# Ten-token group moved to the end of the order, with its first matmul in one pass of seven products

## The chip, the cores and the metric

One Trainium2 chip, one core of it. The metric is the device time of one execution in microseconds (us). Of the kernel before, three runs were timed: 951.03, 950.65 and 1230.56, median 951.03.

## The reference

The input x has 8 batches of 4224 tokens of 192 features. A causal convolution of seven taps runs along the tokens; its weights are softmaxed and shared by 24 features (eight heads). Then comes a block that normalizes each token, multiplies by 192x768, takes the relu, multiplies by 768x192 and adds the result to its input:

```python
w = np.exp(weight - max); w = w / (sum(w) + 1e-09)
out[b, s, h, :] = sum_k w[h, k] * x_pad[b, s + k, h, :]      # K = 7, zeros ahead of each batch
xn = (x - mu) / np.sqrt(var + 1e-06) * g_ln                  # x is now out
return x + np.maximum(xn @ w_ch1, 0.0) @ w_ch2
```

All is float32.

## The kernel before

**Groups.** The 33792 tokens lie on 128 partitions in 264 columns, and the work goes in 18 groups of columns. Group 0 has 6 columns of batch 0, group 1 the 8 columns that are left over of all batches, group 2 the next 10 columns of batch 0, and groups 3 to 17 have J = 16 columns each. The list is `groups` (L70).

**One group.** Its x is loaded with six earlier tokens a partition (`load_x`, L133; two buffers). The first tap is a multiplication on ScalarE (ACT, `first_tap`), the second one too, into a tile of its own that DMAs of the POOL queue add to y (`second_tap`, `add_second_tap`, L400 to L407). The other taps are multiply-adds on VectorE (DVE), one for each tap and head (`conv`, L409, 40 in a group). DVE turns y round in 32x32 blocks (`transpose`, yt) and takes its moments. GpSimd (POOL) works out the root of the variance for two groups at a time (`root`, chained by `chain_of`), in a generator whose halves are put between other POOL work. y is stored to the output, and the block's result is later added to it there by accumulating DMAs (`add_to_out`).

**The first matmul ("up").** Groups 0 to 2 go through `up` (L559): for each of six blocks of 128 hidden features, 24 matmuls with 32x128 weights, four side by side, evicted by ACT with the relu. Groups 3 to 17 go through `up_mixed` (L617), which splits both operands in quarters and makes seven products of quarters instead of eight. It does so in two passes, `one` over one block of features a half and `two` over two, with two sets of four PSUM banks, X and Y, by turns. Each pass starts on the set that the other pass did not end with, so pass two starts and ends on Y. The products need sums of quarters: of the weights (`w1sums`, made once by POOL), and of y (`sums_of_y`, L599: two by DVE, two by POOL). Evictions are on ACT, additions into already evicted quarters are DMAs of the POOL queue or DVE additions from PSUM (`close`, L662 to L670; the last of them, of c21, is DVE's L666). The taps of the next group stand on DVE's queue between these (`taps_of_next`, L744 to L777).

**The second matmul ("down").** Groups 0 and 1 go through `down` (L798), with 128x128 weights. From group 2 on, `down_fast` (L842) makes seven products over as many columns as `fast` gives: 10 in group 2, 16 in the full groups, 12 in the last one, whose other four columns are plain (`down_row`, L796). The half sums for it are written over the quarters that they are made of (`half_sum`). ACT work of the next groups is put behind its products (`work`, `behind`).

**The order around the change.** It is written out by hand in the loop at the end (L1016 to L1085). Every engine runs its instructions in the order in which they are issued, and so do the DMA queues of SP and POOL. At L1026 to L1062 the first three groups are woven together: during group 0 the taps of groups 1 and 2 are begun, the load of group 3 goes out on SP (`load_x(3, gate=True)`, L1041), then eight stores of group 1 (`store_y(1)`). During group 1 DVE makes group 2's ten columns (`conv(2, 2)`, L1047), POOL makes `w2sums` (L1051 to L1054), and group 3 is begun. During group 2's first matmul DVE makes most of group 3's taps (L1058, L1060). In the last group the evictions of pass one are shared by ACT and DVE (L648 to L656), and the group before is scaled by DVE (L731 to L736).

Of the kernel before, what the change touches and what calls it, by code (L numbers as in the profile page):

```python
# [16 lines left out]
def kernel(  # L17
# [52 lines left out]
    groups = [(0, 0, 6), (None, 0, LEFT), (0, 6, J - 6), (0, J, J)]  # L70
    groups += [(b, j0, J) for b in range(1, B) for j0 in (0, J)]
    assert PAD <= 6 and max(n for _, _, n in groups) <= J
# [3 lines left out]
    fast = {g: groups[g][2] if g >= 3 else 0 for g in range(NG)}  # L76
    fast[NG - 1] = J - 4
    fast[2] = groups[2][2]
# [3 lines left out]
    MIXED = range(3, NG)  # L82
    PAIR = NF // 2 - 1
    HJ = J // 2
    EARLY = 10
# [47 lines left out]
    def load_x(g, queue=nc.sync, pad=True, gate=False):  # L133
# [21 lines left out]
        if b:  # L155

            queue.dma_start(
                out=flat[:, 0 : (PAD + n) * D],
                in_=bass.AP(
                    tensor=x.tensor, offset=(b * S - PAD) * D, ap=[[R * D, P], [1, (PAD + n) * D]]  # L160
                ),
            )
            if pad:
                nc.gpsimd.memset(t[0:1, 0:PAD, :], 0.0)
            return
# [215 lines left out]

    def second_tap(g, heads=(0, H)):

        n = groups[g][2]
        if heads[0]:
            pass
        elif g == 2:
            part = upool.tile([P, 3 * HJ * CH * C], F32, tag="ys", name="tb2")
            tb[g] = part[:, 0 : n * D].rearrange("p (j d) -> p j d", d=D)
        elif g == 3:  # L390
            tb[g] = room[:, (NF * NQ * C - D) * J :].rearrange("p (j d) -> p j d", d=D)
        else:
            tb[g] = bpool.tile([P, J, D], F32, tag="tb", name=f"tb{g}")
        for h in range(*heads):
            cs = slice(h * GRP, h * GRP + GRP)
            nc.scalar.mul(tb[g][:, 0:n, cs], xg[g][:, 1 : 1 + n, cs], taps[:, h, 1:2])  # L396
        if heads[1] == H:
            add_second_tap(g)

    def add_second_tap(g, upto=H):  # L400
        n = groups[g][2]
        step = 4 if upto == H else 8
        for js in (slice(j, min(j + step, n)) for j in range(0, n, step)):
            ends = [v[:, js, 0 : upto * GRP] for v in (y[g], tb[g])]
            if upto == H:
                ends = [v.rearrange("p j d -> p (j d)") for v in ends]
            nc.gpsimd.dma_start(out=ends[0], in_=ends[1], accum_op=ALU.add)  # L407
# [24 lines left out]
    def chain_of(g):  # L432


        return g - g % 2 if g < 3 else g - 1 + g % 2
# [55 lines left out]
    def hidden_tile(g):  # L491
        n = groups[g][2]

        if fast[g]:
            ht[g] = room.rearrange(
                "p (h e f q j t) -> p h e f q j t", h=2, e=2, f=FC, q=NQ, t=width(g)
# [10 lines left out]
    def evict_up(g, f, src):  # L507

        if not fast[g]:
            dst = ht[g][:, f].rearrange("p j q t -> p q j t")  # L510
            src = src.rearrange("p q (j t) -> p q j t", t=C)
        elif width(g) == C:
            dst = of_products(g)[:, :, f // FC, f % FC].rearrange("p h q j t -> p q h (j t)")
            src = src.rearrange("p q (h w) -> p q h w", h=2)
        else:
            dst = ht[g][:, :, f // FC, f % FC].rearrange("p h q j t -> p q j h t")
            src = src.rearrange("p q (j h t) -> p q j h t", h=2, t=T)
            for q in range(NQ):
                nc.scalar.activation(dst[:, q], src[:, q], AF.Relu)
            return  # L520
        nc.scalar.activation(dst, src, AF.Relu)  # L521
# [23 lines left out]
    def between(g, f):  # L545

        if g == 1 and f > 2:
            second_tap(3, heads=[(0, 2), (2, 5), (5, 6)][f - 3])
        elif g == 2:
            if f == 0:  # L550
                scale(0, 0, groups[0][2])
                add_to_out(0, 0, groups[0][2])
                nc.gpsimd.memset(xg[4][0:1, 0:PAD, :], 0.0)
            elif f == 2:
                add_to_out(1, 0, groups[1][2])
            elif f > 2:
                first_tap(4, heads=[(0, 3), (3, 6), (6, 7)][f - 3])
# [34 lines left out]
    def quarters_of_y(g):  # L592
        if width(g) == C:
            cuts = [(slice(HJ * h, HJ * h + HJ), slice(0, C)) for h in range(2)]
        else:
            cuts = [(slice(0, J), slice(T * h, T * h + T)) for h in range(2)]
        return [yt[g][:, js, CH * k : CH * k + CH, ts] for js, ts in cuts for k in range(2)]

    def sums_of_y(g, engine):  # L599
# [3 lines left out]
        s1, s2, s3 = [room[:, v] for v in range(3)]  # L603
        a11, a12, a21, a22 = quarters_of_y(g)
        ysums[g] = s1, s2, s3, a21
# [6 lines left out]
        engine.tensor_tensor(a21, a12, s2, op=ALU.subtract)  # L612
# [4 lines left out]
    def up_mixed(g, ahead, pending):  # L617
# [3 lines left out]
        last = g + 1 == NG  # L621
# [5 lines left out]
        done = groups[g - 1][2]  # L627

        class Pass:
            def __init__(self, f0, f1, chain, other):  # L630
                self.n, self.chain, self.other = f1 - f0, chain, other
# [14 lines left out]
            def evict(self, banks, dst, relu=False, f=None):  # L646
                src = self.seen(banks, f)
                if last and self.n == 1:  # L648
                    near, far = [[v[:, :, q : q + 2] for v in (dst, src)] for q in (0, 2)]
                    if relu:  # L650
                        nc.scalar.activation(*near, AF.Relu)
                        nc.vector.tensor_scalar_max(*far, 0.0)
                    else:
# [462 lines left out]
```

## Time and profile before

The profile is of one execution on core 0.

| | |
|---|---|
| span of the profiled execution | 948.1 us |
| median of the runs | 951.03 us, 2.9 above that span |
| granted TensorE clock, mean | 1.000 |
| DVE taps, L415, 128x384 | 602, pace 0.53 us |
| group 2: first matmul, second matmul on PE | 19.59, 17.43 us |
| full group: first matmul, second matmul | 27.61, 27.33 us |
| last group: second matmul of 12 columns, four plain columns | 20.73, 8.01 us |
| last DVE instruction starts | 944.03 us |
| accumulating DMA y<-tb, 384 KB, issue to landing | 8.4 us median |
| load of x of a full group, 2112 KB, issue to landing | 16.2 us median |

In the lines of the profile, PE is the matmul engine and PEld its weight loads, DVE is VectorE, ACT is ScalarE, POOL is GpSimd, SP the queue that issues DMAs. L531 is every matmul of `up` and `up_mixed`, L859 every one of `down_fast`, L796 every one of `down_row`. Each matmul stands in the records twice, so 252 matmuls are 504 records. A line of a timeline has start, duration, engine, line, operation, out<-in, shapes and count, and in brackets the idle time before it with what ended it.

### The profile page before, as it was taken

The numbers are of one execution on the slowest core, as the hardware profiler recorded it, in microseconds if no ns is written. First come the engines' busy times: TensorE is split into PE (matmuls) and PEld (weight loads), VectorE is DVE, ScalarE is ACT, GpSimd is POOL, SyncE is SP. The second block draws the span as 40 slices with busy tenths as digits, with TensorE's granted clock in tenths as the row PEclk, the third lists the DMA queues.
The fourth block names the chain that finished last, engine by engine and source line by source line (L and its number), as shares of the span: only waits on it lengthen the run. The fifth ranks groups of instructions, "written<-read, shape, count | busy, mean of one in ns | idle before, by whom it ended". The sixth has DMA issues, their size and how long they took to land.

```text
span 948.1 us, 38092 instructions
## 1 busy us (share of the span) xinstructions
PE 940.8 (99%) x16910; PEld 751.7 (79%) x16910; DVE 893.7 (94%) x1498; ACT 699.8 (74%) x1250; POOL 342.7 (36%) x478
## 2 busy tenths in 40 slices
PE   8999999999999999999999999999999999999998
PEld 7998896877869687786968898696877869696787
DVE  8999999999999999999999999999999999999867
ACT  6764678596877969687896968779696877867362
POOL 2158422723145141533227141452316341261420
PEclk9999999999999999999999999999999999999999
DMA  8359589689797988979698896969889797778261
GB/s 222 97 151 220 102 235 274 121 190 231 135 270 134 252 162 188 220 132 279 126 252 151 199 221 127 282 131 251 162 194 213 131 274 136 174 137 131 54 114 68
DMA packets 39833, 169.35 MB, mean 179 GB/s; under 512 B 4469, under 2 KB 8182, under 8 KB 33655
## 3 DMA queue, kind: packets, MB, share of 16 engines
q0 software_dynamic: 32992, 107.46, 61.1%
q1 hardware_dynamic: 6672, 59.47, 17.0%
q8 instruction: 132, 2.16, 0.9%
q14 instruction: 31, 0.25, 0.1%
q10 hardware_dynamic: 6, 0.00, 0.0%
HBM read 38.93 MB, written 50.33 MB: 94 GB/s over the span
## 4 chain that ended last, share of the span: by engine, by line
PE 96%; DMA 2%; POOL 1%; ACT 1%; issue 0%; SPq 0%; DVE 0%; ACTq 0%; POOLq 0%
PE ps L531 46%; PE ps L859 44%; PE ps L796 4%; DMA xg<-in_x_dram 1%; DMA room<-room 1%; PE ps L326 1%; ACT room L660 0%; POOL room L615 0%; PE ps L352 0%; POOL d L458 0%; ACT w L360 0%; ACT room L521 0%; POOL r L481 0%; POOL d L476 0%; POOL d L477 0%
## 5 line engine op out<-in xcount | busy, mean ns | idle before, releaser
L415 DVE SCALAR_TENSOR_TENSOR y<-xg,taps,y 128x384 f32<-128x384 f32 (+3 forms) x720 | 364.2, 581 | 2.4 <-DMA y<-room 1.9
L859 PE MATMUL ps<-room,w2sums 128*32 128x256 f32 (+2 forms) x4608 | 245.5, 371 | 0.2 <-issue 0.2
L531 PE MATMUL ps<-yt,w 32*128 32x256 f32 (+2 forms) x4160 | 237.6, 373 | 0.1
L531 PEld LDWEIGHTS ps<-yt,w 32*128 32x128 f32 x4160 | 210.3, 185 | 21.9 <-issue 7.0
L859 PEld LDWEIGHTS ps<-room,w2sums 128*32 128x32 f32 x4608 | 154.7, 110 | 84.9 <-issue 0.8
L660 ACT COPY room<-ps 128x512 f32<-128x512 f32 (+1 forms) x213 | 174.2, 859 | 62.9 <-PE ps L531 62.4
L859 PE MATMUL ps<-room,w 128*32 128x256 f32 (+2 forms) x3456 | 189.2, 371 | 0.0
L826 DVE TENSOR_TENSOR room<-room 128x1024 f32<-128x1024 f32 (+2 forms) x147 | 161.2, 1169 | 21.5 <-PE ps L859 11.1
L859 PEld LDWEIGHTS ps<-room,w 128*32 128x32 f32 x3456 | 113.9, 110 | 67.2 <-DVE room L666 5.0
L531 PE MATMUL ps<-ysums,w1sums 32*128 32x256 f32 x2160 | 127.0, 376 | 0.2 <-issue 0.2
L531 PEld LDWEIGHTS ps<-ysums,w1sums 32*128 32x128 f32 x2160 | 116.2, 185 | 5.4 <-issue 0.6
L949 POOL DMA_DIRECT2D out_dram<-ot x69 | 59.0, 940 | 162.8 <-ACT ot L938 159.2
L865 ACT COPY cs<-ps 128x256 f32<-128x256 f32 (+2 forms) x192 | 70.3, 368 | 45.1 <-PE ps L859 45.0
L407 POOL DMA_DIRECT2D y<-tb x59 | 52.2, 1375 | 137.8 <-ACT room L865 104.6
L673 ACT ACTIVATE room<-room 128x1024 f32<-128x1024 f32 (+1 forms) x89 | 94.4, 1073 | 2.9 <-DMA room<-parts_cs 2.8
L938 ACT ACTIVATE ot<-ot,r 128x192 f32<-128x192 f32 x224 | 94.7, 468 | 0.0
L378 ACT ACTIVATE y<-xg,taps 128x384 f32<-128x384 f32 (+3 forms) x141 | 73.0, 607 | 0.5 <-DMA xg<-in_x_dram 0.5
L446 DVE BATCH_NORM_STATS2 st<-y 128x6 f32<-128x192 f32 x264 | 70.1, 343 | 0.0
L531 PE MATMUL ps<-yt,w1sums 32*128 32x256 f32 x1080 | 68.9, 376 | 0.1
L865 ACT COPY room<-ps 128x256 f32<-128x256 f32 (+2 forms) x96 | 35.4, 370 | 45.0 <-PE ps L859 44.1
L531 PE MATMUL ps<-ysums,w 32*128 32x256 f32 x1080 | 68.3, 374 | 0.0
L396 ACT ACTIVATE tb<-xg,taps 128x384 f32<-128x384 f32 (+1 forms) x120 | 66.1, 628 | 0.0
(120 smaller groups left out, 935.7 us busy)
## 6 DMA issues: line engine op xcount, KB each, us to landing
xg<-in_x_dram SPq DMA_DIRECT2D x14, 2112.0 KB, 16.2
room<-room POOLq DMA_DIRECT2D x45, 512.0 KB, 5.2
out_dram<-ot POOLq DMA_DIRECT2D x59, 384.0 KB, 9.3
y<-tb POOLq DMA_DIRECT2D x58, 384.0 KB, 8.4
out_dram<-y SPq DMA_DIRECT2D x13, 1536.0 KB, 9.4
room<-parts_cs POOLq DMA_DIRECT2D x28, 512.0 KB, 6.9
room<-parts_tb POOLq DMA_DIRECT2D x14, 1024.0 KB, 7.6
xg<-in_x_dram POOLq DMA_DIRECT2D x1, 2112.0 KB, 13.5
```

What stands on the lines that cost most here:

```text
L378: nc.scalar.mul(y[g][:, 0:n, cs], xg[g][:, 0:n, cs], taps[:, h, 0:1])
L396: nc.scalar.mul(tb[g][:, 0:n, cs], xg[g][:, 1 : 1 + n, cs], taps[:, h, 1:2])
L415: nc.vector.scalar_tensor_tensor(out=y[g][:, 0:n, cs], in0=t[:, k : k + n, cs], scalar=taps[:, h, k : k + 1], in1=y[g][:, 0:n, cs], op0=AL ...
L446: nc.vector.bn_stats(out=sums[g][:, j, :], in_=y[g][:, j, :])
L531: nc.tensor.matmul(banks[:, q, i * w + j1 * t : i * w + j2 * t], right[rows, c, P * i : P * i + P], left[rows, j1:j2, c, :], start=start, ...
L660: nc.scalar.activation(to, of, AF.Relu) if relu else nc.scalar.copy(to, of)
L673: nc.scalar.activation(c, c, AF.Relu)
L826: nc.vector.tensor_tensor(a[:, *dst, f], a[:, *left, f], a[:, *right, f], op=op)
L859: nc.tensor.matmul(dst[C * q : C * q + C, 0:w], right[:, f, C * c : C * c + C], left[:, f, q], start=(first and f == PAIR), stop=(f == PAI ...
L865: nc.scalar.copy(to[:, c], dst[:, 0:w].rearrange("p (j t) -> p j t", t=t))
L938: nc.scalar.mul(ots[g][:, j, :], ots[g][:, j, :], rstd[g][:, j : j + 1])
L949: nc.gpsimd.dma_start(out=rows[:, d0:d1], in_=src[:, d0:d1], accum_op=ALU.add)
```

## The change

**Order.** The ten-column group leaves place 2 and becomes the last group, 17. So the full groups follow the second group at once: group 2 is now (batch 0, second half), group 3 is (batch 1, first half), and so on to group 16. `chain_of` and the place where `root` is started are adapted to the new pairs.

**Start.** Group 2 now has 16 columns and goes through `up_mixed`. Its second and third taps are both made by ACT (the third into the tile `third`, behind the copies of `down(0)`), the third is added to the second by four DMAs of the POOL queue, and DVE adds their sum to y in one addition after its four taps. `w1sums[2]`, the y sums and w12 - w11 are made ahead of `down(1)`; the last y sum and `w2sums` stand on POOL's queue behind what `down(1)` issues. The first tap of group 3 and part of its second stand behind the last two blocks of `up(1)`, the rest of the second tap and the scaling of group 0 behind evictions of `down(1)`. On SP, group 1's eight stores go ahead of the load for group 3, which is now three transfers with its zero rows set beforehand.

**End.** The last group has a function of its own, `up_last`: seven products over all three blocks of a half at once, 160 wide, with X and Y by turns (seven products, so the last is on X); ACT evicts, DVE closes all three sums from PSUM. Eight columns go through the second matmul's seven products (128 wide), two are plain. Its half sums are written to free memory (`other`, `room[:, 0:size]`) instead of over their operands.

```diff
-    groups = [(0, 0, 6), (None, 0, LEFT), (0, 6, J - 6), (0, J, J)]
+    groups = [(0, 0, 6), (None, 0, LEFT), (0, J, J)]
     groups += [(b, j0, J) for b in range(1, B) for j0 in (0, J)]
+    groups += [(0, 6, J - 6)]
-    fast = {g: groups[g][2] if g >= 3 else 0 for g in range(NG)}
-    fast[NG - 1] = J - 4
-    fast[2] = groups[2][2]
+    fast = {g: groups[g][2] if g >= 2 else 0 for g in range(NG)}
+    fast[NG - 1] -= 2
...
+    def third_tap(g, heads):
+        if heads[0] == 0:
+            third[g] = cpool.tile([P, J, D], F32, tag="cs", name=f"third{g}")
+        tap_products(g, third[g], 2, heads)
         if heads[1] == H:
+            add_in_parts(g, tb[g], third[g])
...
+        if g == 1 and f == 4:
+            first_tap(3, heads=(0, 3))
+        elif g == 1 and f == 5:
+            first_tap(3, heads=(3, H))
+            second_tap(3, heads=(0, 2))
...
+    def up_last(g, ahead, pending):
...
+        X, Y = take_set(), take_set()
+        product(X, a11, b11, True, False)
+        nc.scalar.copy(c11, seen(X))
+        for step in range(2):
+            next(pending, None)
+        next(ahead)
+        product(Y, a12, b21)
+        close(c11, Y)
+        size = groups[g - 1][2]
+        for j1 in range(0, size, HJ):
+            part, factor = ots[g - 1][:, j1 : j1 + HJ], rstd[g - 1][:, j1 : j1 + HJ]
+            nc.vector.tensor_tensor(
+                part, part, factor.unsqueeze(2).to_broadcast([P, HJ, D]), op=ALU.mult
+            )
+            add_to_out(g - 1, j1, j1 + HJ)
+        product(X, s2, t[0], False, False)
+        nc.scalar.copy(c21, seen(X))
+        product(Y, s3, t[1], True, False)
+        nc.scalar.copy(c22, seen(Y))
+        nc.scalar.activation(c11, c11, AF.Relu)
+        product(X, s1, b12, False, False)
+        close(c22, X)
+        product(Y, a22, t[2], False)
+        close(c21, Y)
+        product(X, s4, b22, False)
+        nc.scalar.activation(c22, c22, AF.Relu)
+        nc.scalar.activation(c12, seen(X), AF.Relu)
+        lower_sum(g, (PAIR, *range(PAIR)))
...
     def down(g):
...
             if g == 0:
                 nc.scalar.copy(ot[:, j : j + 2, :], bank)
+                if j:
+                    third_tap(2, (0, 4) if j == 2 else (4, H))
                 continue
...
+            if j == 0:
+                scale(0, 0, groups[0][2])
+                add_to_out(0, 0, groups[0][2])
+            elif j < 6:
+                second_tap(3, heads=(2, 5) if j == 2 else (5, H))
...
+            store_y(1)
+            load_x(3, apart=True, gate=True)
             moments(0)
             moments(1)
-            load_x(3, gate=True)
-            store_y(1)
...
-        elif g == 1:
-            conv(2, 2)
+        if g == 1:
+            conv(2, 3)
+            flat = [v.rearrange("p j d -> p (j d)") for v in (y[2], tb[2])]
+            nc.vector.tensor_tensor(flat[0], *flat, op=ALU.add)
+            let_in(w1sums[:, 2])
+            sums_of_quarters(w1sums[:, 2], w21, w1sums[:, 0])
             transpose(2)
-            first_tap(3)
-            add_second_tap(3, 6)
+            fourth_sum = sums_of_y(2, nc.gpsimd)
+            nc.vector.tensor_tensor(w12, w12, w11, op=ALU.subtract)
+            moments(2)
+            down(g)
+            fourth_sum()
             sums_of_quarters(w2sums[:, 2], b12, b22)
             sums_of_quarters(w2sums[:, 0], b12, b11)
             sums_of_quarters(w2sums[:, 1], b22, w2sums[:, 0])
             sums_of_quarters(w2sums[:, 3], b21, w2sums[:, 1])
```

## Prediction

> **What bounds the kernel now.** First the page's busy table and the chain that ended last: TensorE (PE) is busy 99% of the span and holds 96% of the chain. Then the chain in order of time, to see whether anything but PE ever ends it:
>
> ```profile
> PE 940.8 (99%) x16910; PEld 751.7 (79%) x16910; DVE 893.7 (94%) x1498; ACT 699.8 (74%) x1250; POOL 342.7 (36%) x478
> PE 96%; DMA 2%; POOL 1%; ACT 1%; issue 0%; SPq 0%; DVE 0%; ACTq 0%; POOLq 0%
> 64.01 15.80 PE ps L796 x96
> 79.81 19.59 PE ps L531 x288
> 99.40 17.43 PE ps L859 x504
> 116.83 3.81 PE ps L531 x63
> ...
> 172.36 27.61 PE ps L531 x504
> 199.97 27.33 PE ps L859 x504
> ...
> 887.67 27.59 PE ps L531 x504
> 915.26 20.73 PE ps L859 x504
> 936.00 8.01 PE ps L796 x48
> 944.01 0.02 issue
> 944.03 0.42 DVE y L953
> ```
>
> A full group costs 27.61 + 27.33 = 54.94 us of PE, back to back. Group 2 (ten columns) starts at 79.81, group 3 at 116.83, group 17 at 887.67: 770.84 us for 14 full groups, 1.7 more than 14 x 54.94 (0.6 of it in group 3's first matmul). The granted clock is full in every slice. So PE's own work and the few places where PE waits decide.
>
> DVE is the engine right behind it. Its timeline in group 4 (start 172.36) shows how close:
>
> ```profile
> 177.59 1.90 DVE L923 STREAM_TRANSPOSE ot<-cs 128x512 f32<-128x512 f32 x3
> 179.41 14.87 DVE L415 SCALAR_TENSOR_TENSOR y<-xg,taps,y 128x384 f32<-128x384 f32 x28
> 195.33 1.67 DVE L415 SCALAR_TENSOR_TENSOR y<-xg,taps,y 128x384 f32<-128x384 f32 x3
> 197.50 2.29 DVE L666 TENSOR_TENSOR room<-room,ps 128x2048 f32<-128x2048 f32 x1 [0.50 <-PE ps L531]
> ```
>
> The next group's taps begin 7.1 us after the group's PE start and run ahead of the close of c21 (L666) on DVE's queue. That close ends at 199.79; PE reuses its PSUM set at 199.97. DVE idles only 0.50 us before it, so taps that start over 0.5 us later make PE wait at the second matmul. From the taps' start to the close's end are 19.9 us of DVE work.
>
> **The change part by part.** All times of the new order keep this execution's zero.
>
> *PE work.* Out go group 2's two matmuls (19.59 + 17.43), the old last group's second matmul (20.73) and its four plain columns (8.01): 65.76. In come one more full second matmul (27.33), the first matmul of ten columns as seven products, the second of eight, and two plain columns. Seven products are 252 matmuls, 504 records, 126 sets of four side by side. The second matmul of 160 wide (17.43 for 126 sets) is 138 ns a set, so 160 wide in the first gives 17.2, if its 32x128 weight loads keep up; the nearest row with these loads, group 0's, is 192 wide: 8.08 us for 48 sets, 168 ns, which as a floor would give 21.2. I take 17.2, since 168 ns fits 192 columns just as 138 fits 160. At 128 wide the nearest row is L365: 28 matmuls in 3.39 us, 121 ns; ends 111 (0.87 of 128 columns) and 121, so 14.0 to 15.2; I take 14.1. Two plain columns: 12 of 334 ns, 4.0. In: 27.3 + 17.2 + 14.1 + 4.0 = 62.6. Net **-3.2**.
>
> The nearest 128-wide row runs at 0.87 to 0.95 ns a column, hardly above 0.86 at 160. The Trainium skill (TensorE: Matmul & The Clock Gate, Back-to-back issue gap) speaks against narrow matmuls: with weight loads in the stream, 128 columns take about 81 ns where the bare matmul takes 56. By that ratio, 1.45, the last second matmul would take 20 us instead of 14, and the sum would rise by 6; I go by the row.
>
> *The end.* Before: second matmul done at 936.00, span end 948.1, 12.1 us, of which 8.0 are rows. After: DVE has the last add, three transposes (0.37 each, from 0.50 at 384 and 0.43 at 320 elements) and eight adds of 0.34, done 4.2 after the second matmul; PE's rows take 4.0, so DVE is late by little: two adds of 0.42, then the store and what follows, 3.65 as before: 8.5. Against 12.1 with 4.0 fewer of rows: **+0.4**.
>
> *The new last group's first matmul.* It has seven products of 2.45, one eviction each. ACT copies 1920 elements in 1.76 (1.87 at 2048), DVE closes in 2.15 (2.29 at 2048). DVE ends the moments of ten columns 0.5 before PE's start, turns group 16 round (5.7, as at 173.77 to 179.4), closes c11 at 7.35; product 4 wants that set at 7.35. The scaling of group 16 (two of 1.71, L733) waits for the root, some 20 POOL instructions, 7.2 us, and ends near 11; the close of c22 wants DVE at 12.3. So no wait inside. But seven products alternate X and Y and end on X, and the second matmul's first bank is X's: it waits for the relu of c12, one ACT instruction over all of X. In the full groups the last product is on Y and this cover does not exist here. Price: 1.76 + 0.1, **+1.9**; ends 0 (if only a bank is waited for) and 4 (if ACT still has the 1.8 us relu of c22 ahead).
>
> *The start, where group 2 is now full.* The work before it is on ACT, DVE, POOL and SP. ACT: 16 taps of 0.53 from 37.13 to 45.6, then down(0)'s copies and the third taps to 51.4; up(1)'s first bank is full at 51.0 and its set wanted again at 53.5: no wait. SP: eight stores (0.42 each) now go ahead of the load of x for group 3, which so starts near 50, as before (51.0); landing 59 to 66 (16.2 us median elsewhere); ACT wants it at 62.5 for three taps that stand before up(1)'s last eviction: 0 to 3.5 us of PE wait, later covered by the next step. DVE:
>
> ```profile
> 47.23 3.69 DVE L446 BATCH_NORM_STATS2 st<-y 128x6 f32<-128x192 f32 x14
> 51.16 15.66 DVE L415 SCALAR_TENSOR_TENSOR y<-xg,taps,y 128x240 f32<-128x240 f32 x40 [0.24 <-DMA y<-tb]
> 66.92 2.18 DVE L426 STREAM_TRANSPOSE yt<-y 128x1920 f32<-128x1920 f32 x1
> ```
>
> Now 32 taps of 0.531 (17.0), 2 more where POOL's w1sums run beside them, to 70.0; the add of tb, 3072 elements, 3.3 (1.14 at 1024, 1.71 at 1536); transpose 3.4 to 76.8; two sums 1.9 to 78.7. Group 2's PE start is 79.8: covered by 3. The third taps' four DMAs, issued by 58.6, land before 70.
>
> Four of the old rows show POOL against DVE: between 72.1 and 76.5 a tap took 1.15 us, not 0.53, while w2sums (L588) ran. The Trainium skill (SBUF — State Buffer, Who interferes with whom) says that a DVE instruction with two SBUF inputs contends with a POOL one that reads SBUF. By it the third y sum on POOL and the w12 subtraction on DVE, issued together at 78.7, hold each other up; by its full block one waits 1.3 us, without it none.
>
> *The wait that is added.* POOL's queue is in order: after w1sums it holds the third y sum (from 78.7, 1.83, 2.3 with the neighbour), then group 0's two output DMAs (1.8), and only then the four DMAs that add group 3's second tap, though ACT has that tap at 78.6. They are issued from 82.8 to 86.4. Landing:
>
> ```profile
> 108.04 3.57 POOL L407 DMA_DIRECT2D y<-tb x4 [4.94 <-ACT tb L396]
> ```
>
> There the transfers' packets ended at about 118, 6.5 after the last issue (8.4 is the page's median). So group 3's y is ready at 92.5 to 94.8; I take 93.3. DVE has been free since 84.5 (moments) and idles; then 19.9 us to the close of c21, 113.2. PE wants that set at 79.8 + 27.6 = 107.4. **+5.9**; ends 2 (POOL's neighbour free, landing 4 us after the issue, the minimum of this line) and 10 (landing 10.3, like the rows out of room, and two taps slowed). It absorbs the wait for x. The fourth sum (86.4 to 88.2) is wanted at 87.7 and w2sums run in DVE's idle time to 92.3; were DVE early, they would cost it 2.5. The 0.6 of the old group 3 goes: **-0.6**. DVE then has 1.85 us of idle a full group, and the order inside full groups is unchanged, so nothing is carried on.
>
> *Nothing or little:* storing y of group 2 by POOL (the old code does it for group 3), output adds of group 1 behind the second matmul's first copies (POOL is idle there), load of x for group 4 from SP (wanted 40 us later), the roots' pairing (two groups each as before).
>
> **Sum:** -3.2 + 0.4 + 1.9 + 5.9 - 0.6 = +4.4. Profiled span 948.1 to 952.5. The median of the runs, 951.03, stands 2.9 above that span; I add the 4.4 to it: **955.5**.
>
> **Rivals.**
> 1. *Group 3's second tap lands early enough* (other side: not slower). It needs y ready by 87.4; for it speaks that ACT is done at 78.6, against it POOL's order. Then +5.9 becomes 0 and the time is 949.6; with no bank wait 947.7. It decides when POOL's four DMAs are issued by about 79.
> 2. *More stands still than I see:* the first matmul of ten is held by weight loads (+4.0), or x for group 3 lands after 68 and pushes the whole start (1 us each). For it: loads are busy 26 of 27.6 us in a full first matmul; against: group 0's pace. 959 to 964.
> 3. *The delay is carried on:* DVE's taps meet POOL's sums in every full group. 40 taps slower by 80 ns are 3.2 us, less 1.85 of idle time: 1.35 a group, 14 groups 19 us, 975. Against: the order inside is the same.
> 4. *No effect:* waits and gains cancel, 951; a part of the first two.
>
> **How the numbers follow.** About 2% (19 us) is what a measurement of this kernel can tell from no change. My forecast (951 to 959) 0.60, rival 1 (947 to 951) 0.18, rival 2 0.17, rival 3 0.04, something that gains over 2%: 0.01, since all exchanged PE work is 3 us. Range: 947 to 963, which leaves out rival 3, the end of rival 2 and the low tail. Faster 0.01, same 0.95, slower 0.04.
>
> **What would show it.** In the changed profile: PE idle or PEld waiting for DVE's L666-like close at the start of group 2's second matmul, some 6 us, with DVE idle near 84 to 93 for a DMA into y; PE idle 1.9 us for ACT between the last group's two matmuls; full groups still 54.94; the last 8.5 us as told. Wrong if group 2 starts much after 82, if full groups grow, or if the 160-wide sets take more than 140 ns.

## The result and the profile after

The changed kernel takes 962.22 us (median of four runs: 965.22, 962.47, 960.28, 961.97), the kernel before 951.02 beside it (median of four, with one run of 1230.56 that the ratio leaves out). The ratio is 1.012 (95% interval 1.010 to 1.014): 11.2 us slower, where 4.4 were forecast. The range held the time, and it is within the 2% called "same". It lies where the second rival was put (959 to 964), but not for that rival's reasons: the weight loads cost 0.95 at most (below), and in the profiled execution PE waits nowhere for x. That the range held it is luck.

The profiled execution is the longest of the four: span 963.4 against 948.1 before and 952.5 forecast. Each of the four runs is 1.8 longer than its span. In the page's busy table, TensorE (PE) is still busy 98% of the span:

```profile
PE 945.3 (98%) x17106; PEld 751.3 (78%) x17106; DVE 892.4 (93%) x1479; ACT 715.6 (74%) x1271; POOL 344.0 (36%) x463
```

A share so high hides 15 us, so the stretches have to be read one by one. First the end, in the chain that ended last (columns: start, duration, engine and line):

```profile
891.75 27.33 PE ps L856 x504
919.09 18.15 PE ps L520 x504
937.24 0.02 issue
937.26 1.78 ACT room L776
939.04 0.04 issue
939.08 15.63 PE ps L856 x504
954.71 4.11 PE ps L796 x24
958.82 0.03 issue
958.85 0.42 DVE y L953
```

The new last group is here as the forecast drew it: 18.15 for the first matmul, then ACT's relu of c12 alone on the path for 1.78, then the second matmul and 8.7 to the end. Only the 15.63 stands out. Now the start, PE's timeline (a bracket is PE's idle time and what ended it):

```profile
80.85 2.02 PE L520 MATMUL ps<-yt,w 32*128 32x128 f32 x34
83.40 1.34 PE L520 MATMUL ps<-yt,w 32*128 32x256 f32 x17 [0.54 <-ACT ot L812]
...
106.92 2.87 PE L520 MATMUL ps<-yt,w1sums 32*128 32x256 f32 x48 [2.17 <-ACT room L634]
...
117.71 7.02 PE L856 MATMUL ps<-room,w 128*32 128x256 f32 x72 [5.33 <-DVE room L640]
```

The forecast wait is there, 5.33 for DVE's close at the start of group 2's second matmul, and two things that were not forecast: 2.17 for ACT inside the first matmul (0.54 more at its start), and a product that takes 7.02 where it takes 4.09 in every full group. The busy times by stretch say why (columns: window, its length, busy us of PE, PEld, DVE, ACT, POOL with their instructions, granted clock of PE, DMA share, GB/s):

```profile
113.00:117.00 4.00, 0.00 (x0) 0.00 (x0) 4.00 (x5) 1.33 (x1) 2.28 (x3) 0.98 1.15 208
117.00:120.00 3.00, 2.29 (x24) 1.14 (x28) 2.90 (x3) 0.00 (x0) 0.00 (x0) 0.50 0.88 94
120.00:123.00 3.00, 3.00 (x36) 1.39 (x32) 3.00 (x7) 1.33 (x2) 0.26 (x1) 0.50 0.95 153
123.00:127.00 4.00, 4.00 (x76) 2.10 (x72) 3.87 (x5) 2.56 (x5) 0.49 (x1) 0.91 0.72 196
```

PE does nothing from 113 to 117, and then works at half its clock until 123.7. The page's row of clock digits shows 9 in every slice; such a stretch is too short for it. The same happened once more, from 939.5 for 3.4 us, in the last second matmul.

Stage by stage, the span against the forecast (each us from the starts above; group 3 starts at 147.98):

| stage | forecast | measured |
|---|---|---|
| up to group 2's start | 79.8 | 80.85 |
| group 2 (54.94 of work) | 60.8 | 67.13 |
| groups 3 to 16 | 770.2 | 771.1 |
| last group, first matmul | 17.2 | 18.15 |
| wait between the matmuls | 1.9 | 1.84 |
| last group, second matmul | 14.1 | 15.63 |
| rest | 8.5 | 8.67 |
| span | 952.5 | 963.4 |

So 6.3 of the 10.9 that were missed lie in group 2, and the rest is small change. What made DVE late there is seen in three queues. POOL's:

```profile
80.19 2.86 POOL L595 TENSOR_TENSOR ysums<-yt 128x768 f32<-128x768 f32 x1 [2.82 <-DVE ysums L594]
83.00 1.80 POOL L949 DMA_DIRECT2D out_dram<-ot  x2
84.17 4.17 POOL L406 DMA_DIRECT2D y<-tb  x4
86.35 3.82 POOL L596 TENSOR_TENSOR yt<-yt,ysums 128x768 f32<-128x768 f32 x1
...
93.36 2.63 POOL L599 DMA_DIRECT2D room<-room  x3
```

The order is the one that was forecast: y sum, group 0's output, then the four transfers that add group 3's second tap. But `w2sums` then keep POOL until 93.4, and the transfers of the closes (room<-room) are issued behind them. What makes these late is the queue: by the trace's landing records the tap's four transfers land at 91.80, 93.69, 95.56 and 97.46 and the closes' three at 99.94, 102.42 and 104.91, one behind the other without a gap. DVE's timeline:

```profile
81.29 4.25 DVE L445 BATCH_NORM_STATS2 st<-y 128x6 f32<-128x192 f32 x16
97.84 14.90 DVE L414 SCALAR_TENSOR_TENSOR y<-xg,taps,y 128x384 f32<-128x384 f32 x28 [12.30 <-issue]
112.66 1.22 DVE L834 SCALAR_TENSOR_TENSOR room<-room 128x1024 f32<-128x1024 f32 x1
113.79 1.67 DVE L414 SCALAR_TENSOR_TENSOR y<-xg,taps,y 128x384 f32<-128x384 f32 x3
115.38 2.28 DVE L640 TENSOR_TENSOR room<-room,ps 128x2048 f32<-128x2048 f32 x1
```

Group 3's taps start at 97.84, not at 93.3; from there to the close's end are 19.8 us, as forecast (19.9). The profile names no releaser for the 12.30; what DVE lacks is y, which is being added to until 97.46. And ACT's timeline:

```profile
74.66 1.12 ACT L383 ACTIVATE tb<-xg,taps 128x384 f32<-128x384 f32 x2 [5.51 <-DVE w1sums L568]
...
81.11 1.63 ACT L383 ACTIVATE tb<-xg,taps 128x384 f32<-128x384 f32 x3
...
105.01 1.87 ACT L634 COPY room<-ps 128x2048 f32<-128x2048 f32 x1 [2.54 <-DMA room<-room]
```

Two waits here were not in the forecast. ACT's second tap of group 3 stands 5.51 us because its tile `tb` has one buffer, which DVE reads until 74.6 (the L1051 addition; the releaser named is the next instruction on DVE). And at 105.01 the copy of c22 waits for the late transfers; that is PE's 2.17.

### The profile page after: what moved, and what is told of

Same layout as the page of the kernel before. It is cut to its first block, busy times and chain, and to the rows that moved or that the text cites. A ratio compares the mean times of both kernels' runs of the same rounds, so it can differ in the third digit from the quotient of the medians.

```text
span 963.4 us, 38488 instructions
## 1 busy us (share of the span) xinstructions
PE 945.3 (98%) x17106; PEld 751.3 (78%) x17106; DVE 892.4 (93%) x1479; ACT 715.6 (74%) x1271; POOL 344.0 (36%) x463
## 5 line engine op out<-in xcount | busy, mean ns | idle before, releaser
L856 PE MATMUL ps<-room,w2sums 128*32 128x256 f32 (+1 forms) x4464 | 243.1, 376 | 0.0
L520 PE MATMUL ps<-yt,w 32*128 32x256 f32 (+3 forms) x4092 | 226.3, 365 | 1.0 <-ACT ot L812 0.5
L856 PE MATMUL ps<-room,w 128*32 128x256 f32 (+1 forms) x3456 | 194.6, 379 | 7.6 <-DVE room L640 5.7
L899 DVE TENSOR_TENSOR room<-room 128x1024 f32<-128x1024 f32 x135 | 154.6, 1218 | 19.1 <-PE ps L856 11.1
L520 PE MATMUL ps<-ysums,w1sums 32*128 32x256 f32 (+1 forms) x2304 | 132.2, 371 | 0.0
L862 ACT COPY cs<-ps 128x256 f32<-128x256 f32 (+1 forms) x192 | 70.9, 369 | 56.8 <-PE ps L856 56.4
L647 ACT ACTIVATE room<-room 128x1024 f32<-128x1024 f32 x90 | 94.8, 1063 | 4.1 <-DMA room<-parts_cs 4.1
L520 PE MATMUL ps<-yt,w1sums 32*128 32x256 f32 (+1 forms) x1152 | 71.9, 372 | 2.8 <-ACT room L634 2.8
L520 PE MATMUL ps<-ysums,w 32*128 32x256 f32 (+1 forms) x1152 | 71.2, 369 | 0.0
L862 ACT COPY room<-ps 128x256 f32<-128x256 f32 (+1 forms) x96 | 35.5, 371 | 44.0 <-PE ps L856 43.4
```

Of the source, the lines that this page charges most:

```text
L520: nc.tensor.matmul(banks[:, q, i * w + j1 * t : i * w + j2 * t], right[rows, c, P * i : P * i + P], left[rows, j1:j2, c, :], start=start, ...
L647: nc.scalar.activation(c, c, AF.Relu)
L856: nc.tensor.matmul(dst[C * q : C * q + C, 0:w], right[:, f, C * c : C * c + C], left[:, f, q], start=(first and f == PAIR), stop=(f == PAI ...
L862: nc.scalar.copy(to[:, c], dst[:, 0:w].rearrange("p (j t) -> p j t", t=t))
L899: nc.vector.tensor_tensor(dst[:, f], left[:, f], right_of[:, f], op=op)
```

## The experiments

All kernels start from the changed one, if nothing else is said; their times stand against runs of the kernel before on the same chip (medians 949.8 to 950.6 where several were taken). The taps of group 3 can be late by ACT's wait for `tb` (the first theory) or by POOL's order and what its queue carries (its rival). Beside this stands the question whether the lower clock is a consequence of PE's idle time, wherever that comes from.

**A second place for the second tap (the buffer alone).**

```diff
-            tb[g] = bpool.tile([P, J, D], F32, tag="tb", name=f"tb{g}")
+            if g == 2:
+                tb[g] = room[:, (NF * NQ * C - D) * J :].rearrange("p (j d) -> p j d", d=D)
+            else:
+                tb[g] = bpool.tile([P, J, D], F32, tag="tb", name=f"tb{g}")
```

> The second tap of group 2 gets memory of its own (the unused end of room), so that ACT needn't wait for DVE's addition before it writes group 3's second tap; all else as in the changed kernel. Theory A (ACT's 5.5 us wait for the buffer is the cause): group 3's taps on DVE start at about 92 instead of 97.8, PE's 5.3 us wait at group 2's second matmul falls to under 0.5, the stretch at half clock after it goes, and the median falls by 9 to 12, to 950 to 953. Theory B (POOL's order is the cause: the third y sum stands ahead of the DMAs that add the tap): ACT is 5 us earlier, but the DMAs still go out from about 84; DVE's taps start at 97 to 98, the wait stays at 5, and only the 0.5 us at the first product goes: 960 to 962.

Measured: 962.17, ratio 1.013 [1.011, 1.014]. ACT no longer waits there, and nothing is gained:

```profile
81.08 2.85 POOL L598 TENSOR_TENSOR ysums<-yt 128x768 f32<-128x768 f32 x1 [2.82 <-DVE ysums L597]
83.88 1.79 POOL L952 DMA_DIRECT2D out_dram<-ot  x2
85.05 4.15 POOL L409 DMA_DIRECT2D y<-tb  x4
...
99.02 14.91 DVE L417 SCALAR_TENSOR_TENSOR y<-xg,taps,y 128x384 f32<-128x384 f32 x28 [12.59 <-ACT parts_cs L637]
```

The transfers are issued as late as before, behind POOL's sum. That the buffer alone makes the taps late falls. PE's waits are spread otherwise, which theory B did not expect: 4.21 for c22 and 1.93 at the second matmul, instead of 2.17 and 5.33.

**The third and fourth y sums of group 2 on DVE (POOL's order alone).** `sums_of_y(2, nc.vector)()` in the place of the sum on POOL, and no `fourth_sum()` behind `down(1)`.

> The third and fourth y sums of group 2 are made by DVE (0.95 us each) instead of POOL, so that POOL's queue is free for the DMAs; the buffer is shared as in the changed kernel. Theory A: ACT's taps end at 82.7 as before, so the DMAs go out from 82.7 instead of 84.2, and DVE's taps start 1 to 2 earlier: the median falls by 1 to 2, to 960 to 961. Theory B: the wait falls by 4 or more and the clock stays: 950 to 955.

Measured: 960.02, ratio 1.010 [1.008, 1.013]. The transfers are issued at 83.31, behind ACT's tap; the taps start at 94.91, PE waits 4.80. The median is near the 960 to 961 that theory A expected here, while the edit before went as theory B had it: neither is the cause alone.

**Both.**

> Both edits together. If A and B are two gates in a row (each hides behind the other, at 82.7 and 83.0), only this one opens the way: the DMAs go out from about 77, group 3's taps start on DVE at 87 to 90, PE's wait at group 2's second matmul is under 1.5, the half clock there goes, and the median is 950 to 953. If the landing of the DMAs is slow for another reason (the load for group 4, the output adds beside them), the taps start at 92 or later and the median stays over 955.

Measured: 959.86, ratio 1.010 [1.008, 1.011]. The transfers are issued at 80.42, the taps start at 93.44, PE waits 3.74 and still falls to the half clock. Part of the gain in issue time, 3.75, is lost: DVE's w12 subtraction now takes 3.76 instead of 1.35, beside `w2sums` on POOL, which began 0.39 after it, and the transfers still land late, as the second alternative had it. The two rows:

```profile
82.61 4.01 POOL L574 TENSOR_TENSOR w2sums<-w 128x288 f32<-128x288 f32 x2
82.22 3.76 DVE L1059 TENSOR_TENSOR w<-w 128x1152 f32<-128x1152 f32 x1
```

**Group 0's output additions behind the tap's transfers.**

```diff
             if j == 0:
                 scale(0, 0, groups[0][2])
-                add_to_out(0, 0, groups[0][2])
             elif j < 6:
                 second_tap(3, heads=(2, 5) if j == 2 else (5, H))
+                if j == 4:
+                    add_to_out(0, 0, groups[0][2])
```

> In the changed kernel, only the two DMAs that add group 0's result to the output are moved on POOL's queue behind the four that add group 3's second tap. Theory D (accumulating DMAs move 0.2 MB/us whatever their number, so 0.59 MB of output ahead of the tap's 1.57 MB costs 3 us of landing): the four go out from 83.1 and land by about 92.5; DVE's taps start 4 to 5 us earlier than 97.8, PE's wait at group 2's second matmul falls by 4 to 5, the half clock there mostly goes: median 955 to 958. Rival (the POOL issue alone counts, 1.8 us): taps start at 96, median 960 to 961.

Measured: 957.95, ratio 1.008 [1.006, 1.010], the best of the single edits. In its timeline:

```profile
83.05 3.54 POOL L406 DMA_DIRECT2D y<-tb  x4
85.28 3.09 POOL L950 DMA_DIRECT2D out_dram<-ot  x2
...
94.86 14.90 DVE L414 SCALAR_TENSOR_TENSOR y<-xg,taps,y 128x384 f32<-128x384 f32 x28 [9.30 <-issue]
108.86 4.28 PE L520 MATMUL ps<-yt,w1sums 32*128 32x256 f32 x48 [4.08 <-ACT room L634]
```

The transfers go out 1.1 earlier and the taps start 3.0 earlier (4 to 5 were expected). So it is not only the place on POOL's queue that counts: the 0.59 MB of output additions ahead hold the DMA engines. The wait at the second matmul is gone; PE's one long wait is now the 4.08 for c22, behind the closes' late transfers, and the product after it takes 4.28 at a clock that is half for 3.4 us. That this wait grew through the edit is not shown: the kernel with swapped sets (below), whose start is that of the changed kernel, has 4.32 there and 0.94 at the second matmul, where the changed kernel has 2.17 and 5.33. But what the late taps covered is now the limit.

**The whole tap early.** Both edits of the y sums and the buffer; the rest of the second tap behind the first eviction of `down(1)`, group 0's scaling and output behind the second, and the w12 subtraction ahead of the y sums.

```diff
             if j == 0:
+                second_tap(3, heads=(2, H))
+            elif j == 2:
                 scale(0, 0, groups[0][2])
                 add_to_out(0, 0, groups[0][2])
-            elif j < 6:
-                second_tap(3, heads=(2, 5) if j == 2 else (5, H))
```

> On top of the two edits of the third experiment (buffer apart, y sums on DVE): all of group 3's second tap is made by ACT behind the first eviction of the plain second matmul, group 0's output is scaled and added behind the second one, and the subtraction w12 - w11 goes ahead of the y sums on DVE. Theory D: the tap's DMAs go out from 75 with nothing ahead of them and land by 85; DVE goes from the moments (end 88) straight to the taps; PE's wait at group 2's second matmul is under 1 and the clock stays full: median 952 to 955. Rival (something else holds the taps or the close): taps start after 92, wait over 3, median over 957.

Measured: 956.16 over ten runs (950.6 to 960.7), ratio 1.006 [1.004, 1.008], above the 952 to 955 that were expected. In the profiled execution, span 949.9 and the second shortest of the ten, group 2 is nearly whole:

```profile
75.45 3.52 POOL L409 DMA_DIRECT2D y<-tb  x4
...
87.94 14.88 DVE L417 SCALAR_TENSOR_TENSOR y<-xg,taps,y 128x384 f32<-128x384 f32 x28
...
107.80 4.09 PE L859 MATMUL ps<-room,w 128*32 128x256 f32 x72 [0.81 <-DVE room L643]
```

DVE goes from the moments to the taps without idling, PE waits 0.81, the clock stays full, and group 2 takes 55.8. So the chain of transfer, tap, close and second matmul is the cause of what this stage lost. The median gets back 6.1 of the 11.2, and the runs spread by 10 us, where those of before spread by 2 to 3.

**Filler matmuls in PE's idle time (for the clock).** Fourteen matmuls into a free bank ahead of group 2's second matmul.

> 14 matmuls of 128x128 by 128 columns into a PSUM bank that the second matmul doesn't use, put between group 2's two matmuls: they add nothing to the result and run while PE would wait (about 3.1 us of the 5.3). Theory C (the half clock after the wait comes of PE's idleness): the granted clock stays 1.0 there or the stretch is halved, the first product takes 4 to 5.5 instead of 7.0, and the median falls by 1.5 to 3 to 959 to 960.5. Rival (the clock falls for another reason, or an idle time of 2 us is enough): the stretch at 0.5 stays 3.4 or 6.8 us long and the time is 961 to 964.

Measured: 962.80, ratio 1.013 [1.011, 1.015]. In the profiled run (957.8) the clock stays full and the product takes 4.09; the filler takes 3.39 and 2.00 of idle time is left. The three other runs have mean clocks of .995 to .997, as without filler, and the median lies where the rival had it. So this trial doesn't decide, and the clock needed a cleaner one.

**Idle time put into the kernel before (for the clock).**

```diff
             taps_of_next(5, 6, heads=(H // 2, H - 1))
+            for _ in range({6: 1, 9: 2, 12: 3, 15: 4}.get(g, 0)):
+                nc.vector.tensor_scalar_max(y[g + 1], y[g + 1], -3.0e38)
         p.close(p.c21, X)
```

> The kernel before, with one, two, three and four extra DVE passes over the next group's y (a maximum with a value far below all of y, so nothing changes in it) in groups 6, 9, 12 and 15, ahead of the close of c21. Each pass takes 1.6 to 3.2 us, so that PE stands still at the start of the second matmul of these groups for about one to four passes less 0.5. Theory E (idle time of PE lowers the granted clock): after the longer of these idle times the clock is at 0.5 for 3.4 or 6.8 us, as it is in the changed kernel, and the time grows by the idle time plus 1.5 to 3 us for each; the kernel before, which never had it, then shows it. Rival (the lower clock belongs to the changed code or its place in the program): clock 1.0 throughout, and the time grows by the idle times alone, some 15 to 30 us.

Measured: 968.21, ratio 1.021 [1.019, 1.023]; span 966.3, 18.2 above that of before. PE's timeline at the four places:

```profile
310.91 4.09 PE L861 MATMUL ps<-room,w 128*32 128x256 f32 x72 [1.08 <-DVE room L666]
...
478.68 4.09 PE L861 MATMUL ps<-room,w 128*32 128x256 f32 x72 [2.61 <-DVE room L666]
...
648.36 5.53 PE L861 MATMUL ps<-room,w 128*32 128x256 f32 x72 [4.67 <-DVE room L666]
...
821.32 6.08 PE L861 MATMUL ps<-room,w 128*32 128x256 f32 x72 [6.63 <-DVE room L666]
```

After 1.08 and 2.61 us of idle time the product takes 4.09; after 4.67 it takes 5.53, after 6.63 it takes 6.08. The idle times sum to 15.0; the products are longer by 1.4 and 2.0, which is the rest of the 18.2 within 0.3. So the clock follows idle time, and not the changed code.

**The sets of the last group swapped** (`Y, X = take_set(), take_set()` in `up_last`).

> In the changed kernel, only the two PSUM sets of the last group's first matmul change places, so that its last product is on the set whose banks the second matmul takes last. If the 1.87 us of PE wait there is the bank (as forecast): the wait falls to under 0.6, and with it the chance of a half clock in the second matmul; median 1.5 to 3 lower, 959 to 961. If it is the relu itself or DVE's half sums: the wait moves to a later product and the time stays, 961 to 964.

Measured: 962.11, ratio 1.013 [1.010, 1.015]. The 1.87 turns into pieces, in PE's timeline:

```profile
917.46 5.17 PE L520 MATMUL ps<-yt,w 32*128 32x160 f32 x144 [0.49 <-ACT cs L862]
...
937.47 0.86 PE L856 MATMUL ps<-room,w 128*32 128x128 f32 x24 [0.42 <-ACT room L776]
939.76 3.80 PE L856 MATMUL ps<-room,w2sums 128*32 128x128 f32 x131 [1.01 <-issue]
```

They sum to 1.92. The reason that was given for the wait (the set of the last product is the set that is wanted next) is right; taking it away gains nothing, since PE then stands 1.01 with no releaser named and waits for ACT at the group's start.

**The half sums of the last group over their operands, as before.**

> In the changed kernel, only the half sums of the last group are written over their operands again, as before the change, instead of to free memory. If the free memory matters, DVE must wait for PE's third and fourth products before it may write, and PE waits for DVE at the fifth product: 1 to 2 us more, 963 to 965. If the wait is hidden (DVE's nine sums of 0.63 run beside products of 2.0), no difference: 960.5 to 963.5, no new PE wait in the last group.

Measured: 960.49, ratio 1.010 [1.009, 1.012], and no new wait on PE: the free memory makes no difference that shows.

**Early tap and swapped sets together**, and the same kernel profiled twice more, to see where its long runs lose their time.

> The edits of the early tap together with the swapped sets of the last group; nothing is left out. Profiled span of the early tap alone: 949.9, with PE idle of 0.81 at the start and 1.87 in the last group. Theory E (each PE idle time of about 2 us or more may set the granted clock to half for 3.4 us, and that is the spread of 950.6 to 960.7 among the ten runs of the early tap): with the 1.87 us wait split in shorter ones, no PE idle time over 1.1 us is left in the new parts, so the runs gather at 950 to 953, clocks at .999 or more. Rival (the spread comes from somewhere else, such as the length of the transfers at the start): the runs spread as before, median 955 to 957, with clocks from .996 to 1.0. Against the kernel before: Theory E 'same', ratio about 1.000; rival 1.006.

> The same kernel as the one before (early tap and swapped sets), to have the trace of another execution of it; its runs spread from 952.2 to 959.6 while the kernel before spreads by 2. Theory F: a long run (over 955) has group 3's second tap landing late, so that PE waits for DVE's addition at the start of group 2's second matmul, 3 to 6 us, between 105 and 120. Rival: a long run loses it ahead of 80, by the load of x for group 3 landing late (ACT's third wait for xg), and group 2 starts up to 6 us later than the 80.3 or so of the short run. If this run is short again (under 954), neither is told apart.

> The same kernel once more, for the same end: theory F, a wait of 3 to 6 us for DVE at group 2's second matmul in a run over 955; rival, the loss lies ahead of group 2's start.

Measured: 956.40 over six runs (952.2 to 959.6), ratio 1.007 [1.004, 1.009], so the clock after the 1.87 is not the spread. The two further executions were long, spans 959.3 and 957.7, and show neither of the two things that were expected. Group 2's second matmul in the first of them:

```profile
110.19 4.09 PE L859 MATMUL ps<-room,w 128*32 128x256 f32 x72 [0.62 <-DVE room L643]
...
118.82 9.80 PE L859 MATMUL ps<-room,w2sums 128*32 128x256 f32 x122 [3.26 <-issue]
```

Nothing that the profile shows holds PE for 3.26 us; in the other execution it is 2.97. PE's instructions come over the DMA engines, 16 KB at a time: the instruction queue moved 134 such packets for the changed kernel's 34,212 records of matmuls and weight loads, and 132 for the 33,820 of the kernel before, 255 to 256 for each. In the records of these two runs one such packet lands near 106 and the next starts at 116.4 and 115.9; PE goes on 2.4 us later, with the clock at half for 6.8 us around it. In the short execution (951.4) one starts at 107.6 and the next at 118.1, and PE has no such wait.

**Less traffic there.** First the eight output additions of group 1 some ten evictions later, then also y of group 2 stored by SP's queue ahead of group 2 instead of by POOL's in the middle.

> The early tap with swapped sets, and one more edit: the eight output additions of group 1 (0.77 MB through POOL's queue) leave the head of group 2's second matmul, where they follow at once on the partial sums of its first matmul, and stand some ten evictions later. In two long executions of the kernel without this edit (959.3 and 957.7) PE stood still for 3.3 and 3.0 us with no instruction to run, near 115.6, and its next 16 KB of instructions came over the DMA engines at 116.4 and 115.9, after none since 105, while those additions held all DMA engines; the clock then fell to half for 6.8 us. Theory G (instructions of PE come late behind the additions): with the additions later, the instructions come earlier, no idle time of 3 us is left in most runs, clocks .998 or more, the median falls from 956.4 to 951 to 953 and the spread shrinks. Rival (instructions come late for another reason, such as the other traffic, or run to run): median stays at 955 to 957, with clocks of .996 among the runs.

> The kernel with early tap, swapped sets and later additions of group 1, and one more edit: y of group 2 (1.5 MB) is stored by SP's queue, ahead of group 2's products and behind the load of x, instead of by POOL's queue in the middle of its first matmul, where it holds the DMA engines from 98 to 103. Theory H (PE's instructions come late because POOL's queue keeps all DMA engines busy from 93 to 118): with 1.5 MB less there, the 16 KB of instructions that came at 116.8 come before 113, PE has no idle time of 3 us near 115, the clocks are .998 or more and the median falls from 956.9 to 951 to 953. Rival (the traffic is not what holds them up): the idle time of 3 to 4 us for no releaser stays in the profiled run or in the clocks of most runs, median 955 to 958. A loss can come too: the store beside the transfers of group 3's second tap makes PE wait for DVE near 110.

Measured: 956.91 (951.0 to 959.2), ratio 1.006 [1.004, 1.008], with 4.08 us of the same kind in the profiled run: the additions were not it, or not alone.

```profile
119.20 8.57 PE L862 MATMUL ps<-room,w2sums 128*32 128x256 f32 x122 [4.08 <-issue]
```

Then 957.22 (954.9 to 958.7), ratio 1.007 [1.006, 1.009]: its profiled run has at most 0.9 with no releaser named, but pays 2.17 for c22 and 2.31 for the close at the second matmul, since the store now delays the other transfers. Traffic was moved, not taken away, and neither median fell. That late instructions are what holds PE there is inferred from the packets' times, and what holds them up stays open.

## Why the prediction was right and wrong

**Right:** the sign and the place. The work of full groups is unchanged (771.1 for fourteen). The wait at group 2's second matmul comes through POOL's order and group 3's second tap, and the early tap takes it away. The bank wait of the last group is 1.87 (forecast 1.9), its end 8.7 (8.5), and the second matmul of 128 columns takes 14.2 where the clock stays full (126 sets, 113 ns each, in the variant with both edits), as the row said (14.1), not the 20 that was estimated from the ratio in the Trainium skill (TensorE: Matmul & The Clock Gate, Back-to-back issue gap). The wait that was forecast for x of group 3 did not reach PE in the profiled execution; in four variants with the same start PE lost 0.25 to 1.16 us there.

**Wrong: the size of +5.9.** The second matmul of group 2 starts at 117.71, not at 113.2. That the wait itself, 5.33, looks like the forecast 5.9 is luck: PE had already lost 2.17 and 0.54 on the way and came later to it. Three things failed.

1. *"There the transfers' packets ended at about 118, 6.5 after the last issue."* DVE waits for the landing, not for the end of the packets: of those four transfers the last was issued at 109.7 and took 9.5 to land, so 119.2. (In the changed kernel the last one lands at 97.46 and DVE's taps start at 97.84; with group 0's additions moved, 94.49 and 94.86.) And nothing of POOL's stood ahead there. Here 0.59 MB of output additions go ahead of the 1.57 MB of the tap, with the closes' 1.57 MB right behind, and POOL's queue moves no more. The windows of the changed kernel show the limit, all DMA engines busy (share above 1) at 0.21 MB a us:

```profile
84.00:88.00 4.00, 4.00 (x79) 3.83 (x75) 1.54 (x6) 3.27 (x7) 4.00 (x6) 1.00 0.96 133
88.00:92.00 4.00, 3.91 (x67) 3.30 (x67) 0.00 (x0) 2.48 (x6) 3.92 (x5) 1.00 1.11 212
92.00:97.00 5.00, 5.00 (x100) 4.75 (x96) 0.00 (x0) 2.82 (x2) 3.91 (x5) 1.00 1.08 209
```

0.59 MB at this rate are 2.8 us, near the 3.0 that moving them gave back; the forecast had 1.8 of this, as issue time. From the last issue to the taps it had 6.9; 9.5 were measured, and 8.3 with the additions moved. POOL's y sum ended at 83.05, not at 81.0: it began 1.5 later and took 2.86, not 2.3. So of the taps' 4.5, about 2.0 come from the y sum, 1.4 from the landing by itself and 1.2 from the additions.

2. *No step for the closes of group 2's own first matmul.* Their transfers land right behind the tap's, 2.5 us for each 0.52 MB, and the last at 104.91, 0.1 before ACT's copy; so the bytes ahead hold them, and not `w2sums`, behind which POOL issues them. That is the 2.17; it costs nothing more as long as the taps are later still, and takes over when they are not (4.08 with group 0's additions moved). The forecast said that `w2sums` run in DVE's idle time, and did not ask what stands behind the tap on POOL's queue.

3. *No step for the clock.* The sum has no term for it. The stall set PE to half speed for 6.8 us, worth 2.9 in the product after it, and 1.5 in the last group. So a wait of some 5 us costs 8.

Together 4.5 + 2.9 + 1.5 are 8.9 of the 10.9 that were missed. The first matmul at 160 columns is 144 ns a set, not 138 (+0.95), which is past the 140 that the forecast had named as a sign of being wrong, and the groups between grew by 0.9. The start of group 2 is 1.04 late, which is inside the 4.5, since the y sum came later with it. Of this 0.93 is already there when `down(0)` begins: PE's clock became full at 11.06 in this execution and at 6.88 in that of before. Among the variants with the same beginning it became full at 6.2 to 7.6 in five executions and at 11.2 to 12.1 in eight, and the kernel with early tap and swapped sets has both (7.34, then 12.13 and 11.65). So one kernel can have either; of the kernel before there are too few traces to say how often.

**Overlooked, but without effect at first:** the buffer of `tb`. The first edit shows that it was covered by POOL's order; it became the next limit as soon as that was mended (issue at 83.31 with the sums on DVE alone, at 80.42 with both edits). The forecast's two ends for POOL's sum beside DVE's subtraction (held up for none or for the whole 1.3) enclose what came: POOL took 2.86 instead of 1.83, DVE its usual 1.35. The Trainium skill (SBUF — State Buffer, Who interferes with whom) says that the order of issue decides who is held up. That agrees with the changed kernel, where DVE's subtraction starts at 80.02 and POOL's sum at 80.19, but not with the one with both edits, where DVE starts first too, at 82.22 against 82.61, and takes 3.76.

**The offset.** 2.9 was added to the span. Runs are 1.8 longer than their own spans; the other 1.1 was a difference between two executions.

**Open:** which of the undone parts would bring the change to even. The best medians stay 5.6 to 6.5 above before; the shortest runs reach it or nearly (950.59 and 951.04 against 950.6 and 950.3). No variant beat the kernel before.

## What to carry to other kernels

When a transfer is moved to another place on a queue, price it by what lies ahead of it in bytes, at the rate that the queue has when all DMA engines are busy, and not by its landing time somewhere else. Then go through everything that is now behind it on that queue, and ask what is late next. A matmul engine that stands still for some 2 us or more may pay for it a second time at half its clock (after a wait of 2.31 in the last variant above), so a long wait is dearer than short ones of the same sum that lie far apart.

## What the runs showed of the hardware

**The clock goes by fixed windows.** In each of these traces every change of PE's clock lies a whole number of 3.413 us after the first one (in the changed kernel it became full at 11.06, half at 116.88, full at 123.70, half at 939.49 and full at 942.90: 31, 33, 272 and 273 such windows; in the kernel with stalls it fell after 188 and 238). Counting PE's idle time in these windows over the changed kernel and the variants, up to the last matmul (worked out from the starts and lengths of the matmuls):

| idle share of the window before, at full clock | windows | clock half in the next |
|---|---|---|
| 60 to 100% | 13 | 13 |
| 50 to 58% | 10 | 1 |
| below 50% | all others | 0 |

This explains the four stalls: 2.61 fell across a border, 1.17 and 1.45, and cost nothing; 4.67 and 6.63 each covered one window wholly. It also makes a stall of some 2 to 4 us (an estimate, 0.6 to 1.2 of a window) a matter of chance: the windows stand differently in each execution. The Trainium skill (TensorE: Matmul & The Clock Gate, Part 1: The HAM clock gate) has the window, 3413 ns and free-running; it asks for an idle one, and here 60% idle was enough.

**Adding transfers are slow.** POOL's accumulating transfers held all DMA engines at 208 to 212 GB/s (windows above), where the load of x, with the DMA share just above 1, moved 356 to 386 GB/s (118 to 122 in two executions of the kernel with early tap and swapped sets; the higher one is shown). It is not POOL's queue as such: its plain store of y moved 400 GB/s from 109 to 112 in the changed kernel, at a share of 1.01. A byte that is added takes the room of nearly two that are loaded.

```profile
118.00:122.00 4.00, 3.87 (x76) 1.97 (x72) 2.49 (x2) 4.00 (x11) 0.00 (x0) 1.00 1.01 386
```

**PE may run out of instructions** while that traffic lasts: it stood still for 3.0 to 4.1 us in three long executions, with no releaser named, and went on 2.4 us after its next 16 KB of instructions had started to come. That the one is the cause of the other is not shown.
